# Sharing one pass through the output weights between a recurrent memory and its tokens

## The chip, the core and the metric

The kernel runs on one core of one Trainium2 chip. The metric is the time of one execution in microseconds (us) on the device. Each run was timed beside the kernel before on its own chip, and its ratio is to those runs. The experiments lie on three chips (runs 1 to 4, 5 to 8, 9 to 11); the kernel before differs by less than 0.2% between them, but a difference between runs of two groups, or from the changed kernel, is one across chips.

Engine names in the profile: PE is TensorE's matmuls, PEld its weight loads, DVE is VectorE, ACT is ScalarE, POOL is GpSimd, SP is SyncE, which starts most of the transfers here.

Tiles that the profiles name: `psm` holds the projections to queries and keys with which every segment starts, `psv` those to values, `psb` the query and key projections of a block's last tokens (eight per segment), `psS` the scores, `psD` and `psRt` the sums and reciprocals of the softmax, `psOm` and `psOt` the attention's output for memory and tokens, `pw` and `psy` (later `pwB`) the passes through `Wo`. `Rc` is the reciprocal and `PT` the probabilities, both made on DVE.

## The reference, cut to what matters

Two layers are applied twice: a recurrent attention with a small memory, and a gated MLP. All tensors are bf16. The attention is sequential: 64 segments of 32 tokens, and the 8 rows of memory that a segment starts with are the first 8 output rows of the segment before.

```python
# H = 32 heads, Dh = 128, Dm = 512, M = 8 memory rows, seg_len = 32
mem = mem0
for s in range(n_seg):                        # 64 segments, one after the other
    xs = x[:, s * seg_len:(s + 1) * seg_len, :]
    h = jnp.concatenate([mem, xs], axis=1)    # 40 rows
    q, k, v = (einsum('btd,dhe->bhte', h, W) for W in (Wq, Wk, Wv))
    p = softmax(where(mask, q @ k^T * scale, -1e9))
    o = einsum('bhqk,bhke->bhqe', p, v)
    o = einsum('bhte,hed->btd', o, Wo)        # Wo: 32 x 128 x 512
    mem = o[:, :M, :]                         # the next segment waits for this
    outs.append(o[:, M:, :])
...
x = x + A(layernorm(x)); x = x + B(layernorm(x))      # the whole pair twice
```

## The kernel before

Both recurrent stages (one per application of the attention) go through 16 blocks of four segments, 128 tokens to a block. The layer norm of a block is done once, and its rows are brought to the layout with the model dimension on partitions by PE transposes. `hA` holds the 8 memory rows and the first 24 tokens of a segment, `hB` and `hBs` the last 8 tokens.

The memory of a segment goes through `Wo` at once, because the next segment waits for it. The tokens are kept in `oT4` and go through `Wo` a block at a time, as filler work (`fill`) in the next block's segments.

```python
        def gen_block_ln(tb):
            xs = xp.tile([P, DM], F32, name="xs")                 # 2 buffers
            nc.sync.dma_start(xs[:], xd[tb * P:(tb + 1) * P, :])
            yield
            xn = wk.tile([P, DM], BF16, name="xn", bufs=1)
            nc.vector.tensor_scalar(out=xn[:], in0=xs[:], ...)    # layer norm
            ...
            for kt in range(KT):
                nc.tensor.transpose(pT[:, kt, :], xn[:, kt * P:(kt + 1) * P], ident_bf[:])
            ...                                                   # nine copies into hA, hBs, hB
            blk_state[tb] = dict(xs=xs, hB=hB)                    # xs held for gen_y

        def gen_y(tb):                                            # the tokens' pass through Wo
            psy = acc.tile([P, DM], F32, name="psy")
            for h in range(H):
                nc.tensor.matmul(psy[:, :], lhsT=bs["oT4"][:, h, :], rhs=Wo_sb[:, h, :], start=(h == 0), stop=(h == H - 1))
                if h % 4 == 3:
                    yield
            xo = xp.tile([P, DM], F32, name="xo", bufs=1)
            nc.vector.tensor_tensor(out=xo[:], in0=psy[:], in1=bs["xs"][:], op=ALU.add)
            nc.sync.dma_start(xd[tb * P:(tb + 1) * P, :], xo[:])
            _stats(nc, wk, xo[:], MV_out[:, tb, :])               # bn_stats for the next layer norm
```

```python
        # in segment(s): the memory's pass; column tile cg sums the heads h with h % 4 == cg
            for h in range(H):
                cg = h % 4
                nc.tensor.matmul(pw[32 * cg:32 * cg + 32, :], lhsT=uT_cur[:, h, :], rhs=Wo_sb[:, h, :],
                                 start=(h < 4), stop=(h >= H - 4), tile_position=(0, 32 * cg))
            nc.scalar.copy(pw_sb[:, 0:256], pw[:, 0:256])
            nc.vector.tensor_copy(pw_sb[:, 256:512], pw[:, 256:512])
            fill(FILLU)
            ...                                                   # token probabilities
            for kt in range(KT):
                nc.tensor.transpose(pmT[:, kt, :], pw_sb[:, kt * P:(kt + 1) * P], c["ident_f"][:])
            nc.vector.tensor_reduce(out=hA_nxt[:, :, 0:8], in_=...pmT..., op=ALU.add)   # sum of 4 partials
            ...                                                   # psOt, then copies into oT4
```

The softmax here doesn't subtract the row's maximum and nothing guards it: scores larger than these inputs give would overflow.

## Time and profile before

| what | value | from |
|---|---|---|
| time | 2544.65 us, median of 4 runs (2540.74 to 2553.52) | runs on the chip of the changed kernel |
| profiled span | 2520.7 us, of an execution some 22 us below the median | page |
| the two recurrent stages, first psm to last psm | 987.2 and 988.4 us | starts of psm in the trace |
| PE waits over 0.56 us in those stages | 42, together 34.4 us | from one matmul start to the next in the trace, each less 0.31 us |
| weight load and matmul pairs per segment | 332 | count in the trace |

Two rows of the page that the prediction did not use turn out to matter. The first is PE's granted clock in 40 slices, in tenths; the second is a DMA queue with its packets, megabytes, and share of time:

```profile
PEclk9999999999999999996999999999999999999999
...
q8 instruction: 350, 5.73, 1.0%
```

The clock is full except in the change between the stages. The `instruction` queue moved 350 packets; 5.73 MB over 350 is 16.4 KB each. The page's PE has 44,808 weight loads, so 89,616 loads and matmuls; over 350 that is 256.

And the first block of the first stage, in a table by window (window, its length, then busy time of PE, PEld, DVE, ACT and POOL with the count of instructions, then the granted clock, the DMA share and GB/s):

```profile
84.70:140.00 55.30, 53.94 (x1300) 28.06 (x1292) 30.99 (x69) 28.32 (x65) 5.22 (x14) 1.00 0.01 3
```

PE is busy 53.94 of 55.30 us at full clock: the first block runs as well as any later one (it lacks only the psy of a block before it).

### The profile page before, as it was taken

To read this page: it belongs to the slowest core of one execution; us is meant where nothing else is said; L and a number is where in the kernel's file an instruction comes from. 1 tells how busy PE (TensorE), PEld (TensorE's weight loads), DVE (VectorE), ACT (ScalarE), POOL (GpSimd) and SP (SyncE) were. 2 spreads that over 40 slices of the span, in tenths; PEclk is the share of its full clock that TensorE was granted. 3 is DMA by queue.
4 is the path that set the end of the run, shared out by engine and by line. 5 is a ranking of instruction groups with operands and counts; after the bars stand their busy time and mean duration, and the time that the engine had idled before them with its cause. 6 is when DMAs were issued, how large, how long until landed. Compare 5 with 4: busy or idle time off the path is not lost.

```text
span 2520.7 us, 96292 instructions
## 1 busy us (share of the span) xinstructions
PE 2260.2 (90%) x44720; PEld 1210.8 (48%) x44808; DVE 1162.1 (46%) x2582; ACT 986.6 (39%) x2242; POOL 201.5 (8%) x415
## 2 busy tenths in 40 slices
PE   0799999999999999981979999999999999999889
PEld 0344444444444444440754444444444444444466
DVE  2544444444444444460335444444444444444522
ACT  0344444444444444462004444444444444444700
POOL 1200000000000000001240000000000000000022
PEclk9999999999999999996999999999999999999999
DMA  9000000000000000038550000000000000000254
GB/s 366 11 11 11 11 11 11 11 11 11 11 11 11 11 11 11 7 114 229 137 170 11 11 11 11 11 11 11 11 11 11 11 11 11 11 11 23 98 130 105
DMA packets 105618, 107.94 MB, mean 43 GB/s; under 512 B 69776, under 2 KB 79360, under 8 KB 102144
## 3 DMA queue, kind: packets, MB, share of 16 engines
q1 hardware_dynamic: 79520, 46.88, 7.2%
q10 hardware_dynamic: 21728, 30.78, 3.5%
q0 software_dynamic: 3968, 24.12, 2.6%
q8 instruction: 350, 5.73, 1.0%
q14 instruction: 52, 0.43, 0.1%
HBM read 66.11 MB, written 18.87 MB: 34 GB/s over the span
## 4 chain that ended last, share of the span: by engine, by line
PE 76%; DVE 7%; ACT 6%; DMA 5%; issue 4%; POOL 1%; SPq 0%; ACTq 0%; POOLq 0%; DVEq 0%
PE psv L517 18%; PE psm L528 16%; PE pw L589 10%; PE psy L447 9%; PE pg L195 7%; PE psb L428 4%; ACT vs L522 3%; PE psS L549 3%; PE pmT L610 2%; DMA xs<-xd 2%; PE psRt L603 2%; DVE rowsB L436 2%; PE psOm L582 1%; PE py L206 1%; PE psOt L617 1%
## 5 line engine op out<-in xcount | busy, mean ns | idle before, releaser
L517 PE MATMUL psv<-Wv_sb,hBs 128*32 128x512 bf16 x4096 | 535.3, 381 | 0.0
L517 PE MATMUL psv<-Wv_sb,hA 128*32 128x512 bf16 x4096 | 534.6, 381 | 0.0
L531 ACT CAST rows<-psm 128x512 bf16<-128x512 f32 x512 | 300.1, 586 | 315.4 <-PE psm L528 315.4
L522 ACT CAST vs<-psv 128x512 bf16<-128x512 f32 x512 | 300.1, 586 | 153.7 <-PE psv L517 136.8
L528 PEld LDWEIGHTS <-hA 128*32 128x32 bf16 x8192 | 209.9, 97 | 240.3 <-DVE hA L612 25.2
L528 PE MATMUL psm<-Wq_sb,hA 128*32 128x512 bf16 x4096 | 266.3, 380 | 18.6 <-DVE hA L612 18.6
L528 PE MATMUL psm<-Wk_sb,hA 128*32 128x512 bf16 x4096 | 265.3, 379 | 0.0
L589 PE MATMUL pw<-Wo_sb,uT 128*32 128x512 bf16 x4096 | 244.6, 380 | 1.2
L517 PEld LDWEIGHTS <-hA 128*32 128x32 bf16 x4096 | 180.1, 95 | 108.0
L195 PE MATMUL pg<-wspT,z2n 128*128 128x256 bf16 (+1 forms) x1536 | 177.3, 277 | 59.6 <-issue 59.6
L447 PE MATMUL psy<-Wo_sb,oT 128*128 128x512 bf16 x962 | 223.0, 379 | 7.2 <-issue 4.8
L505 DVE STREAM_TRANSPOSE QQ<-rows 128x512 bf16<-128x512 bf16 x256 | 181.5, 709 | 79.2 <-ACT rows L531 74.8
L626 ACT CAST oT<-psOt 128x512 bf16<-128x512 f32 x128 | 75.0, 586 | 365.1 <-PE psy L447 230.2
L505 DVE STREAM_TRANSPOSE KK<-rows 128x512 bf16<-128x512 bf16 x256 | 181.6, 709 | 29.2 <-ACT rows L531 24.5
L195 PEld LDWEIGHTS <-z2n 128*128 128x128 bf16 (+1 forms) x1536 | 151.4, 100 | 85.2 <-issue 67.1
L517 PEld LDWEIGHTS <-hBs 128*32 128x32 bf16 x4096 | 180.1, 95 | 0.0
L447 PEld LDWEIGHTS <-oT 128*128 128x128 bf16 x1024 | 95.1, 98 | 120.5 <-issue 12.7
L490 POOL COPY QQ<-QTB 128x256 bf16<-128x256 bf16 x128 | 49.8, 404 | 1271.8 <-DVE QTB L438 1221.8
L589 PEld LDWEIGHTS <-uT 128*32 128x32 bf16 x4096 | 98.3, 96 | 104.8 <-ACT uT L585 21.8
L592 ACT COPY pw_sb<-pw 128x256 f32<-128x256 f32 x128 | 47.7, 373 | 236.4 <-PE pw L589 236.4
L198 DVE TENSOR_TENSOR gb<-pg,bsp_bc 128x256 f32<-128x256 f32 x96 | 40.7, 424 | 212.1 <-PE pg L195 212.1
L549 PEld LDWEIGHTS <-KK 128*32 128x32 bf16 x8192 | 89.7, 97 | 91.2 <-DVE KK L505 87.1
(104 smaller groups left out, 2540.7 us busy)
## 6 DMA issues: line engine op xcount, KB each, us to landing
xs<-xd SPq DMA_DIRECT2D x48, 256.0 KB, 3.4
xs<-xd ACTq DMA_DIRECT2D x48, 256.0 KB, 5.0
xd<-xo SPq DMA_DIRECT2D x32, 256.0 KB, 2.1
Wq_sb<-in_A_Wq_dram POOLq DMA_DIRECT2D x6, 1024.0 KB, 20.1
Wk_sb<-in_A_Wk_dram POOLq DMA_DIRECT2D x6, 1024.0 KB, 28.5
Wv_sb<-in_A_Wv_dram POOLq DMA_DIRECT2D x6, 1024.0 KB, 20.5
Wo_sb<-in_A_Wo_dram ACTq DMA_DIRECT2D x4, 1024.0 KB, 14.8
Wo_sb<-in_A_Wo_dram POOLq DMA_DIRECT2D x4, 1024.0 KB, 20.2
```

The costliest lines, as they stand in the source:

```text
L195: nc.tensor.matmul(pg[0:fsz, :], lhsT=z2n[:, st_i, f0:f0 + fsz], rhs=wspT[:, st_i, :], start=(st_i == 0), stop=(st_i == NT - 1))
L428: nc.tensor.matmul(psb[32 * cg:32 * cg + 32, :], lhsT=hB[:, kt, :], rhs=qk_rhs(j, kt, cg), start=(kt == 0), stop=(kt == KT - 1), tile_posi ...
L436: nc.vector.tensor_copy(rB[:], psb[:])
L447: nc.tensor.matmul(psy[:, :], lhsT=bs["oT4"][:, h, :], rhs=Wo_sb[:, h, :], start=(h == 0), stop=(h == H - 1))
L505: nc.vector.transpose(out=dst, in_=rows[j][:])
L517: nc.tensor.matmul(psv[32 * cg:32 * cg + 32, :], lhsT=(hA_cur if cg % 2 == 0 else hB_cur)[:, kt, :], rhs=Wv_sb[:, kt, col0:col0 + 512], st ...
L522: nc.scalar.copy(dstv, psv[:])
L528: nc.tensor.matmul(psm[32 * cg:32 * cg + 32, :], lhsT=hA_cur[:, kt, :], rhs=qk_rhs(j, kt, cg), start=(kt == 0), stop=(kt == KT - 1), tile_ ...
L531: nc.scalar.copy(r[:], psm[:])
L549: nc.tensor.matmul(psS[half][64 * g + 32 * part:64 * g + 32 * part + 32, hl8, :], lhsT=KK[:, part, half, 8 * g + hl8, :], rhs=QQ[:, :, hal ...
L589: nc.tensor.matmul(pw[32 * cg:32 * cg + 32, :], lhsT=uT_cur[:, h, :], rhs=Wo_sb[:, h, :], start=(h < 4), stop=(h >= H - 4), tile_position= ...
L626: nc.scalar.copy(oT4[:, 0:16, 32 * j4:32 * j4 + 32], psOt[0][:])
```

## The change

The intent is to let the tokens ride along in the memory's pass. `uT` has 32 columns per head, of which only 8 carried memory; now the other 24 carry 24 tokens of the segment before. For this, a column tile of PE no longer holds a quarter of the heads over 512 output columns, but all heads over a quarter of the output columns: 128 matmuls of 128 columns in place of 32 of 512. The result is 128x128, complete, and in a layout in which one predicated copy and one transpose on DVE make the next `hA`. The model dimension is permuted to fit, and the layer norm's rows go through DRAM to get that layout. The last 8 tokens of each segment get a pass per block (`pwB`). The rest of the token output is put together by transfers and an add on GpSimd.

```diff
+        def wo_pass(po, lhs):
+            for h in range(H):
+                for cg in range(4):
+                    nc.tensor.matmul(po[32 * cg:32 * cg + 32, 0:128], lhsT=lhs[:, h, :], rhs=wo_rhs(h, cg),
+                                     start=(h == 0), stop=(h == H - 1), tile_position=(0, 32 * cg))
+                if h % 8 == 7:
+                    yield
         def gen_block_ln(tb):
-            xs = xp.tile([P, DM], F32, name="xs")
+            xs = xp.tile([P, DM], F32, name="xs", bufs=1)
...
+            nc.sync.dma_start(xn_d[M + tb * P:M + (tb + 1) * P, :], xn[:])
             yield
+            for j4 in range(4):
+                t = prep.tile([P, P], BF16, name="pre")
+                nc.sync.dma_start(t[:], xn_d[t0:t0 + 32, :].rearrange("r (cg c) -> cg r c", cg=4))
+                pre[4 * tb + j4] = t
             yield
-            pT = acc.tile([P, KT, P], BF16, name="pT")            # PE transposes and copies go
+            ...                                                   # preB: the last 8 tokens of each segment
             hB = blkp.tile([P, KT, 32], BF16, name="hB")
+            nc.vector.transpose(out=hB[:].rearrange("p kt r -> p (kt r)"), in_=preB[:])
...
         def gen_y(tb):
-            psy = ...
+            pwB = acc.tile([P, DM], F32, name="pwB")
+            yield from wo_pass(pwB, bs["oB"])
+            ...                                                   # oB_sb, oB_d, loads of xs_y and ot_y
+            nc.gpsimd.tensor_tensor(out=xo, in0=xo, in1=xs[:], op=ALU.add)
+            nc.sync.dma_start(xd[tb * P:(tb + 1) * P, :], xo)
+            _stats(nc, wk, xo, MV_out[:, tb, :])
...
+        def build_hA(s, pw):
+            t = pre.pop(s)
+            if pw is not None:
+                nc.vector.copy_predicated(out=t[:], mask=maskM[:], data=pw[:, 0:128])
+            nc.vector.transpose(out=hA[s % 2][:].rearrange("p kt r -> p (kt r)"), in_=t[:])
...
         # in segment(s)
-            for h in range(H): ...                                # pw 512 wide, pw_sb
+            for _ in wo_pass(pw, uT_cur):
+                pass
+            build_hA(s + 1, pw)
+            store_o(s, pw)
             fill(FILLU)
...
-            ...                                                   # pmT transposes, tensor_reduce into hA_nxt
             psOt = ...
-            nc.scalar.copy(oT4[...]); nc.vector.tensor_copy(oT4[...])
+            for g, cp in ((0, nc.scalar.copy), (1, nc.vector.tensor_copy)):
+                cp(uT_nxt[:, 16 * g:16 * g + 16, 8:32], psOt[g][:, :, 0:24])
+                cp(oB[:, 16 * g:16 * g + 16, 8 * j4:8 * j4 + 8], psOt[g][:, :, 24:32])
```

## The prediction

> **What bounds the kernel now.** I read the busy table and the slices first, then the chain that ended last, then the groups by shape, then the chain in order of time within a few blocks.
>
> ```profile
> PE 2260.2 (90%) x44720; PEld 1210.8 (48%) x44808; DVE 1162.1 (46%) x2582; ACT 986.6 (39%) x2242; POOL 201.5 (8%) x415
> PE   0799999999999999981979999999999999999889
> PE 76%; DVE 7%; ACT 6%; DMA 5%; issue 4%; POOL 1%; SPq 0%; ACTq 0%; POOLq 0%; DVEq 0%
> ```
>
> PE is full in all slices but the start and the change between the two recurrent stages near the middle, and PE holds 76% of the chain. Nothing else is half busy. So a microsecond of PE work taken out of the recurrent stages is worth nearly a microsecond, if no wait opens in its place. Those stages are two times 16 blocks of four segments. The groups that the change touches:
>
> ```profile
> L589 PE MATMUL pw<-Wo_sb,uT 128*32 128x512 bf16 x4096 | 244.6, 380 | 1.2
> L612 DVE TENSOR_REDUCE hA<-pmT 128x32 bf16<-128x128 f32 x128 | 36.5, 285 | 119.0 <-PE pmT L610 119.0
> L610 PE MATMUL pmT<-ident_f,pw_sb 128*128 128x128 f32 x512 | 90.6, 287 | 4.6
> ```
>
> The reader sees that pw costs 8 groups of four column tiles per segment. The psy group (1,024 full matmuls, 962 recorded, 223.0 us busy) is the tokens' own pass through Wo. In order of time, the end of a segment that has no filler work in it:
>
> ```profile
> 642.65 1.94 PE pw L589 x32
> 644.59 0.02 issue
> 644.62 0.38 ACT pw_sb L592
> 645.00 0.04 issue
> 645.04 0.44 PE pmT L610 x2
> 645.48 0.22 PE psOt L617 x10
> 645.70 0.38 PE pmT L610 x2
> 646.08 0.02 issue
> 646.11 0.30 DVE hA L612
> 646.41 0.04 issue
> 646.45 3.64 PE psm L528 x64
> ```
>
> From pw's end to the next segment's psm the chain crosses four engines and takes 646.45 - 644.59 = 1.86 us. The last segment of the block before shows the psy pass:
>
> ```profile
> 658.21 3.19 PE psy L447 x14
> 661.40 0.44 PE pmT L610 x4
> 661.83 0.51 PE psOt L617 x32
> 662.34 0.16 issue
> 662.50 3.42 PE psy L447 x15
> ```
>
> In that stretch psm starts at 602.9, 618.8, 633.2, 646.45 and 665.8. The four segments of a block therefore take 15.9, 14.4, 13.3 and 19.4 us, together about 62.9 us. The 13.3 is the bare segment; the 19.4 holds psy; the 15.9 and 14.4 hold the four psb passes (16 matmuls in 0.87 us each, 3.5 us per block).
>
> [...] (1) [...] the starts of psm show groups of four, 3 to 4 ns apart within a group, and a new group each 216 ns. [...] psS has N=64 and a new weight load for each matmul, and 32 start in 0.24 us, 30 ns per group of four. (2) [...] The trace has 709 ns for 512 columns[...]. (3) [...] The trace has 285 (the reduce above) and 288 (the tensor_tensor on psD); I use 290. [...] (4)[...] The trace has 2.1 us for xd<-xo and 3.4 for xs<-xd on the same queue, so a round trip through DRAM is 5 us or so.
>
> **The change part by part.**
>
> *pw.* 32 matmuls of 512 columns become 128 of 128 columns: 32 groups of four at about 57 ns instead of 8 at 216. 32 x 57 = 1.82 us against 8 x 216 = 1.73. Even, or 0.1 us worse per segment. But it now carries 24 tokens of the segment before in the columns that were zeros, and yields one 128x128 tile.
>
> *psy.* Goes: 32 x 216 ns = 6.9 us per block, all on the path (PE is full around it). In its place the last 8 tokens of each segment, 32 per block, take a pwB pass: 1.8 us per block. Net -5.1, less 4 x 0.1 for pw: -4.7 us.
>
> *pmT, pw_sb, reduce.* Four fp32 transposes per segment (0.4 to 0.8 us of PE on the chain, 0.6 typical) go: 4 x 0.6 = -2.4 us per block. The block's pT transposes (4, 0.34 us) go too, into reads through DRAM.
>
> *The memory chain.* In place of the 1.86 us: predicated copy 0.29, transpose 0.31, three hand-overs of about 0.04 each: 0.72 us, both on one engine. psOt runs beside it (0.57 us in the timeline of PE, and a few tenths before matmuls of another form start). So in a bare segment 1.86 becomes 0.8, of which 0.6 has been counted as pmT. Further gain 0.5 us in the one bare segment of a block; in the others filler already covers the chain.
>
> *LN of the next block.* In the second segment psb waits for hB behind xn and nine small copies on DVE (PE psb waited 38.0 us in 30 places, 1.3 us each). xs no longer is held until psy is done, so the loads can be issued a block early. I take half: -0.6 us.
>
> *Added elsewhere.* About 22 small transfers per block on the SP queue (about 0.4 us of issue each, 9 of 55 us), an output copy on ACT, an add on GpSimd. ACT changes by about +0.05 us per segment: psOt's copy is split (+0.16) and o_sb comes (0.27), pw_sb goes (0.37). DVE is lighter: pw_sb, the reduce and eight hA/hBs copies go. Both stay near half busy.
>
> *Sum per block.* -4.7 - 2.4 - 0.3 - 0.5 - 0.6 = -8.5 us. I give back 0.5 for DVE standing in order behind a landing that comes later than planned (the hB transpose waits for a load, a store and a load). -8.0 x 32 = -256 us.
>
> *Ends.* Each recurrent stage has one more pw pass (1.8 us), and the last block's tokens go through DRAM, about 5 us, before the gMLP stage can take its statistics; against that the exposed psy of the last block (6.9 us) shrinks to 1.8. The first block needs the DRAM trip as well, but the GpSimd memsets covered that time (they end at 79.4 us, psb starts at 79.6). Estimate +3 us per stage, +6 in all. The permuted reads in the gMLP stage keep their element counts; 0.
>
> 2542.6 - 256 + 6 = about **2293 us**; the trace's bare-segment chain may be worth more than I took, so I put the point at **2285**.
>
> **Rivals.** *A: dispatch becomes the bound.* PE gets 240 more instructions per segment, and no burst of small matmuls in this trace is longer than 32, a pw pass is 128. [...] Against it: where a psS burst ends, at 1336.50, psv weight loads follow each other every 8.3 ns, each with its matmul in the stream; a group of four then needs 33 ns, below 57. [...] *C: a DMA wait takes psy's place.* The chain shows it already: DVE stood behind xn with xs landing at 670.97, and KK after it. Two such waits of 1 to 2 us per block would make it 2330 to 2370. For it: three DRAM trips in a row on one queue, and DVE in order. Against: pre has nine buffers and xs is free early, so it can run a block ahead. *D: the predicated copy is slow* (two passes, 0.6 us): +0.3 us per bare segment, +10 us, the rest hidden by filler. *E: DVE or ACT become the bound*: 46% and 39% busy and hardly changed; no.
>
> **Range and chances.** PE's own work alone gives -7.4 per block, about 2305; all waits removed (-9.5 per block) gives 2240; rival C gives up to 2370, of which I keep the lower half. Range 2235 to 2340. Faster by over 2% needs under 2492[...]: 0.96. Within 2%: 0.025. Slower: 0.015.
>
> **What would show it.** pw groups 57 ns apart and a pw pass near 1.8 us; psm about 12.2 us after psm in the bare segment, some 54.5 us per block; DVE predicated copy near 0.29 us and its transpose near 0.31; no psy and pmT rows; PE still near 90%. Wrong if pw's starts spread over 3 us or more (A, B), if DVE's idle time before hB, xn or the predicated copy sums over 60 us with a DMA as its end (C), or if the ends of the two stages cost over 10 us each.

## The result, and the profile after

The changed kernel takes 2446.39 us (median of 4 runs, 2444.18 to 2455.31). The ratio to the kernel before is 0.9626, with a 95% interval of 0.9586 to 0.9667. Ratios here are the mean time of one kernel's runs over the mean of the other's of the same rounds, so not quite the ratio of the medians. The change gains 98 us. The prediction had it gain 258, and its range ended at 2340: the direction was right, the time was 161 us above the point and outside the range.

The page of the changed kernel, rows of busy time, slices, clock, the instruction queue, and the chain that ended last:

```profile
PE 2063.5 (84%) x59776; PEld 1267.5 (52%) x59776; DVE 1111.9 (46%) x2425; ACT 987.0 (40%) x2404; POOL 270.3 (11%) x577
PE   0599999998999999773967988988899899997799
PEclk9999999999999999986989999999999999999899
...
q8 instruction: 467, 7.65, 1.3%
...
PE 63%; DMA 11%; DVE 9%; issue 7%; ACT 6%; SPq 2%; POOL 2%; ACTq 0%; POOLq 0%; DVEq 0%
```

PE has 197 us less work, but is down from 90% to 84%, and its share of the chain from 76% to 63%. DMA and "issue" have grown in the chain, and the clock has dips inside the stages. There are 59,776 matmuls and as many loads, 119,552 together, and the instruction queue has 467 packets: 119,552 / 467 = 256 exactly.

The parts themselves came out as predicted. The groups by shape (line, engine, operation, tiles, shape, count, then busy us, mean ns of one, and idle time before them with what ended it):

```profile
L475 PE MATMUL pw<-Wo_sb,uT 128*32 128x128 bf16 x16640 | 280.4, 226 | 34.0 <-issue 31.5
...
L544 DVE STREAM_TRANSPOSE hA<-pre 128x128 bf16<-128x128 bf16 x128 | 39.9, 311 | 4.7 <-DMA pre<-xn_d 0.5
...
L543 DVE CAST_PREDICATED pre<-maskM,pw 128x128 bf16<-128x128 uint16 x126 | 36.7, 291 | 199.3 <-PE pw L475 199.2
```

And the end of a bare segment in the chain (start, length, what), to be held against the six steps of the kernel before that took 1.86 us:

```profile
626.81 2.00 PE pw L475 x128
...
628.83 0.30 DVE pre L543
...
629.16 0.32 DVE hA L544
629.48 0.04 issue
629.52 3.64 PE psm L586 x64
```

From pw's end at 628.81 to the next psm at 629.52 are 0.71 us. So what went wrong lies between the parts. From the starts of psm, the length of each kind of segment (the n-th of a block) in the steady blocks of both stages:

| segment of the block | before, median | after, median (shortest) |
|---|---|---|
| first | 19.4 | 12.8 (12.2) |
| second | 15.8 | 15.0 (14.5) |
| third | 14.6 | 16.8 (15.3) |
| fourth | 13.3 | 14.3 (12.6) |
| sum | 63.0 | 58.9 (54.5) |

The steady blocks are the third to the fifteenth of each stage. The shortest sum to 54.5 us per block, the prediction's number, but in part by chance: the shortest third and fourth segments still hold waits (the tenth run below gets down to 53.4). The changed kernel seldom reaches these lengths. In the kernel before a kind of segment was the same every time, to 0.02 us in the first, third and fourth.

Three things take the time.

**Gaps in which PE waits for nothing that the profile shows.** The chain between two segments that carry filler:

```profile
655.64 0.22 PE psb L457 x4
655.86 0.76 issue
656.62 0.83 PE psb L457 x12
...
658.84 0.39 PE pwB L475 x20
659.24 1.12 issue
660.36 0.80 PE pwB L475 x44
```

PE stops in the middle of a run of identical matmuls, with no operand that the profile shows it waiting for, twice in 5 us (0.76 and 1.12 us). Nearly all gaps of this sort lie at one place in the count of PE's instructions, taken modulo 256: at 186 in the first stage, and 168 in the second. Between the two in this fence, from the gap at 655.86 to that at 659.24, PE issued 12 + 64 + 32 + 20 = 128 pairs, 256 instructions. There are 118 such gaps of 0.3 to 2.2 us in the two stages, together 124 us. 37 of them lie within pw, 34 within pwB, 20 within psOt, 14 within psm, 7 within psb and 6 between two tiles. In the kernel before there is none. The place will be called the mark.

**DVE standing in order.** Three rows of the table of waits (who, for what, us in total, times, longest):

```profile
DVE bnst L99 <- POOL ot_y L498: 88.8, 29, 17.2
...
DVE xn L424 <- DMA xs<-xd: 52.9, 29, 3.7
...
PE psD L632 <- DVE Rc L625: 31.7, 26, 3.0
```

bnst is the statistics of a block's output. It waits on DVE for GpSimd's add, and that add mostly waits for the last transfer into ot_y (22 of 32 times in the same table). What that does to PE, from the chain of one block's fourth segment:

```profile
607.79 1.27 POOL ot_y L498
...
609.08 0.69 DVE bnst L99
...
610.30 0.25 PE psD L632 x2
...
612.66 3.56 PE pw L475 x128
```

The softmax of the segment needs a reciprocal on DVE, which stands behind bnst, which stands behind GpSimd. PE stood still for 2.11 us before that psD. In the table above it waits for Rc 26 times, 31.7 us in all, 1.2 on the mean.

The row of xn is the layer norm. In the first block of the first stage DVE takes 13 of them, 12 of which wait for their load (22.6 us of waits in this window):

```profile
82.30:155.20 72.90, 57.71 (x1664) 33.05 (x1656) 35.63 (x78) 28.11 (x68) 6.86 (x22) 0.91 0.28 82
```

The window holds the four segments of the first block. They take 72.90 us where the kernel before took 55.30, with PE busy in 57.71 only; in the second stage it is 72.3 against 55.3.

**Half clock.** In the fence before last, pw takes 3.56 us, not 2.0. The records of the clock show half speed from 610.96 us for 6.83 us, just after that wait of 2.11 us; over the two stages of the changed kernel it is 64.8 us, and none in the kernel before. The two stages hold 16 such stretches of half clock, 13 of 3.41 us and 3 of twice that, 6.83; 3.41 us is called a window below. By the trace's ends of matmuls PE stood still for 1.1 to 3.0 us in the 3.41 us before each; but other windows with up to 1.8 us were not followed by half clock, so no threshold comes out. Before 13 of the 16 the longest wait of PE lies away from the mark; before the other 3 it is a gap at the mark.

### The profile page after: what moved, and what is told of

Its sections match the earlier page's. It is cut to its first block, busy times and chain, and to the rows that moved or that the text cites. A ratio compares the mean times of both kernels' runs of the same rounds, so it can differ in the third digit from the quotient of the medians.

```text
span 2442.4 us, 127869 instructions
## 1 busy us (share of the span) xinstructions
PE 2063.5 (84%) x59776; PEld 1267.5 (52%) x59776; DVE 1111.9 (46%) x2425; ACT 987.0 (40%) x2404; POOL 270.3 (11%) x577
## 4 chain that ended last, share of the span: by engine, by line
PE 63%; DMA 11%; DVE 9%; issue 7%; ACT 6%; SPq 2%; POOL 2%; ACTq 0%; POOLq 0%; DVEq 0%
PE psv L575 16%; PE psm L586 13%; PE pw L475 11%; PE pg L209 7%; ACT vs L580 3%; PE pwB L475 3%; DMA xs<-xd 3%; PE psb L457 3%; PE psS L607 3%; DMA wspT<-in_B_w_sp_dram 2%; DVE rowsB L465 2%; PE psRt L659 2%; DVE QTB L467 1%; DMA xb<-in_A_x_dram 1%; DMA oB_d<-oB_sb 1%
## 5 line engine op out<-in xcount | busy, mean ns | idle before, releaser
L586 PEld LDWEIGHTS <-hA 128*32 128x32 bf16 x8192 | 219.9, 98 | 238.9 <-issue 29.6
L475 PE MATMUL pw<-Wo_sb,uT 128*32 128x128 bf16 x16640 | 280.4, 226 | 34.0 <-issue 31.5
L586 PE MATMUL psm<-Wq_sb,hA 128*32 128x512 bf16 x4096 | 276.1, 385 | 21.2 <-DVE hA L544 13.2
L475 PEld LDWEIGHTS <-uT 128*32 128x32 bf16 x16640 | 249.9, 100 | 62.0 <-issue 38.8
L586 PE MATMUL psm<-Wk_sb,hA 128*32 128x512 bf16 x4096 | 274.9, 383 | 3.4 <-DVE rowsB L465 1.9
L575 PEld LDWEIGHTS <-hA 128*32 128x32 bf16 x4096 | 180.1, 96 | 109.9 <-issue 2.1
L548 ACT COPY o_sb<-pw 128x128 f32<-128x128 f32 x130 | 34.6, 266 | 352.3 <-DVE pre L543 334.4
L457 PE MATMUL psb<-Wq_sb,hB 128*32 128x512 bf16 x1024 | 71.3, 392 | 101.1 <-DVE hB L441 76.0
L457 PEld LDWEIGHTS <-hB 128*32 128x32 bf16 x2048 | 53.2, 99 | 145.5 <-DVE hB L441 76.0
L543 DVE CAST_PREDICATED pre<-maskM,pw 128x128 bf16<-128x128 uint16 x126 | 36.7, 291 | 199.3 <-PE pw L475 199.2
L673 ACT CAST uT<-psOt 128x384 bf16<-128x384 f32 x128 | 61.5, 480 | 149.0 <-PE psOt L667 149.0
```

The costliest lines, as they stand in the source:

```text
L457: nc.tensor.matmul(psb[32 * cg:32 * cg + 32, :], lhsT=hB[:, kt, :], rhs=qk_rhs(j, kt, cg), start=(kt == 0), stop=(kt == KT - 1), tile_posi ...
L475: nc.tensor.matmul(po[32 * cg:32 * cg + 32, 0:128], lhsT=lhs[:, h, :], rhs=wo_rhs(h, cg), start=(h == 0), stop=(h == H - 1), tile_position ...
L575: nc.tensor.matmul(psv[32 * cg:32 * cg + 32, :], lhsT=(hA_cur if cg % 2 == 0 else hB_cur)[:, kt, :], rhs=Wv_sb[:, kt, col0:col0 + 512], st ...
L586: nc.tensor.matmul(psm[32 * cg:32 * cg + 32, :], lhsT=hA_cur[:, kt, :], rhs=qk_rhs(j, kt, cg), start=(kt == 0), stop=(kt == KT - 1), tile_ ...
L673: cp(uT_nxt[:, 16 * g:16 * g + 16, 8:32], psOt[g][:, :, 0:24])
```

## The experiments

The theories. **Supply**: PE takes instructions faster than a block of 256 of them can be brought, now that each matmul is short. That PE's instructions come in such blocks is read from the instruction queue (350 packets of 16.4 KB before, 467 after, in both 256 of PE's loads and matmuls to a packet); that PE waits for them was conjecture, which e2 and e3 test. **Order**: DVE, in order, stands behind things that need a transfer, and the rest follows from that, half clock included. A third possibility was that the gaps are a matter of the transfers that the change adds.

All the runs passed the comparison with the reference. Two of them compute a wrong value on purpose (they use a wrong slice of the weights); that the comparison did not catch it means that it is a weak check of the attention's part, for the other runs too. Their times are of use, their results are not.

The kernel before, run along with them, had 2545.43 us (runs 1 to 4), 2545.10 (5 to 8) and 2541.79 (9 to 11).

| run | median us | ratio to before (95%) | gaps at the 256 mark: number, us | other PE waits over 0.56 us: number, us | half clock us |
|---|---|---|---|---|---|
| before | 2544.65 | | 0 | 42, 34.4 | 0 |
| after | 2446.39 | 0.9626 (0.9586 to 0.9667) | 118, 124.1 | 42, 54.0 | 64.8 |
| e1_stats_late | 2450.64 | 0.9639 (0.9610 to 0.9668) | 114, 117.4 | 44, 60.0 | 88.7 |
| e2_wo64 (wrong value) | 2339.07 | 0.9200 (0.9164 to 0.9235) | 0 | 49, 75.1 | 88.7 |
| e3_before_pw128 | 2626.91 | 1.0330 (1.0292 to 1.0367) | 66, 59.1 | 37, 28.1 | 34.1 |
| e4_spread_late | 2388.15 | 0.9388 (0.9347 to 0.9429) | 101, 96.4 | 24, 31.0 | 27.3 |
| e5_ln_anchor | 2465.51 | 0.9712 (0.9649 to 0.9775) | 109, 110.8 | 54, 75.8 | 85.3 |
| e6_stats_anchor | 2419.42 | 0.9529 (0.9459 to 0.9599) | 122, 136.0 | 28, 34.3 | 37.5 |
| e7_all3 | 2402.15 | 0.9463 (0.9404 to 0.9522) | 90, 76.4 | 31, 53.8 | 81.9 |
| e8_thin | 2357.04 | 0.9284 (0.9215 to 0.9353) | 80, 74.6 | 23, 24.4 | 34.1 |
| e9_after_all | 2371.01 | 0.9341 (0.9316 to 0.9366) | 125, 123.2 | 3, 1.5 | 6.8 |
| e10_wo64_all (wrong value) | 2237.96 | 0.8812 (0.8782 to 0.8843) | 0 | 6, 4.7 | 6.8 |
| e11_thin_hb | 2306.31 | 0.9093 (0.9055 to 0.9131) | 81, 67.8 | 2, 0.7 | 0 |

The three last columns are counted from the records of one profiled execution each, over the two recurrent stages: a gap is taken as one at the mark when it lies at the place modulo 256 at which most of the gaps between like matmuls of that stage lie. Gaps at the mark are those over 0.3 us from one matmul start to the next, less 57 ns each; other waits are counted from 0.56 us, less 0.31 us each.

### e2_wo64: half as many instructions for the same columns

```diff
         def wo_pass(po, lhs):
-            for h in range(H):
+            for h in range(0, H, 2):
                 for cg in range(4):
-                    nc.tensor.matmul(po[32 * cg:32 * cg + 32, 0:128], lhsT=lhs[:, h, :], rhs=wo_rhs(h, cg), ...)
+                    nc.tensor.matmul(po[32 * cg:32 * cg + 32, 0:256], lhsT=lhs[:, h, :],
+                                     rhs=Wo_sb[:, h:h + 2, :].rearrange("p h (kt g el) -> p g h kt el", kt=4, g=4)[:, cg], ...)
```

The same columns stream through PE, in 64 matmuls of 256 in place of 128 of 128, so the pass has 128 instructions in place of 256 (in the trace of e10, which has the same pass, it takes 1.93 to 1.96 us). The order on the other engines is as before; the sums are wrong.

> Wrong result on purpose. The changed kernel with each Wo pass made of 64 matmuls of 256 columns in place of 128 of 128: the same streaming time (16 groups of 110 ns, 1.76 us), half the instructions. Theory of instruction supply: the gaps at multiples of 256 PE instructions (about 111 us in 112 segments) fall under 40, the time falls by 60 to 110 us to 2336 to 2386. Rival (a wait for DMA and DVE alone explains the loss, or the small matmuls stream slower than 57 ns per group): within 15 us of 2446, or the pw group pace is seen to change.

It took 2339.07 us, 107 less than the changed kernel (2446.39) and within the expected range, and not one gap at the mark is left. The instruction queue has 386 packets, which is 98,816 / 256. This speaks for supply, and against the transfers, which are all still there. The other waits and the half clock grew (75.1 us and 88.7), so the 107 is not all that the gaps cost.

### e3_before_pw128: only the cutting of pw, in the kernel before

```diff
-            for h in range(H):
-                cg = h % 4
-                nc.tensor.matmul(pw[32 * cg:32 * cg + 32, :], lhsT=uT_cur[:, h, :], rhs=Wo_sb[:, h, :], ...)
+            for d4 in range(4):
+                for h in range(H):
+                    cg = h % 4
+                    nc.tensor.matmul(pw[32 * cg:32 * cg + 32, 128 * d4:128 * d4 + 128], lhsT=uT_cur[:, h, :],
+                                     rhs=Wo_sb[:, h, 128 * d4:128 * d4 + 128], ...)
```

The result is right, and nothing else of the change is in it: no added transfers, no moved work on DVE.

> The kernel before with its pw pass cut into four times as many matmuls of 128 columns each, nothing else. Result stays right. Streaming time 32 x 57 = 1.82 us against 1.73. Theory of instruction supply: PE instructions per segment go from about 700 to 890, the densest 256 of them take under 3 us, gaps appear at multiples of 256 instructions; 30 to 90 us slower than before, 2575 to 2635. Rival (128-column matmuls cost only their streaming): 2543 + 12, so under 2560.

It took 2626.91 us, 81 more than the kernel before on the same chip (2545.43), and within the expected range. From the chain:

```profile
636.06 0.30 PE psOt L619 x15
636.36 0.92 issue
637.28 0.39 PE psOt L619 x17
```

A gap within psOt, of the kind seen before, in a kernel that has none of the change's transfers; 66 of them, 59.1 us. So the denser instructions are enough to make the gaps. The pw pass itself takes 1.97 to 2.00 us here, and 1.91 to 1.94 in the kernel before. In the two profiles the stages grew by 73 us: 59 are the gaps, some 8 the longer pass (the shortest bare segment is 13.33 us against 13.27, and there are 128), and 6 are left for the half clock. The rest of the 81 us would lie outside the stages, in parts that this edit does not touch: they took 578 us in this profile and 545 in that of the kernel before, so a difference of this size there can't be read as the effect of an edit.

The half clock came here as well, 34.1 us of it, with no more of other waits than in the kernel before (28.1 us against 34.4). Each of its ten windows had a gap at the mark in the 3.41 us before it. So here half clock followed the gaps.

### e1_stats_late: the statistics a block later, by their place in the program

```diff
-            _stats(nc, wk, xo, MV_out[:, tb, :])
+            late.append(lambda: _stats(nc, wk, xo, MV_out[:, tb, :]))     # run in the next block's second segment
```

> One change to the changed kernel: the statistics of a finished token block (bn_stats on DVE) are emitted one block later, so that DVE does not stand in order behind the GpSimd add. Theory (two losses: DVE behind the GpSimd add, with PE idle and a slower clock after it; and PE running out of fetched instructions): about 1.2 us of wait per block goes, and the half clock after it, so 35 to 70 us less than the changed kernel's 2446: 2376 to 2411; the gaps ahead of the psD matmuls that wait for Rc, 31.7 us by the profile, fall under 5. Rival (only the instruction supply matters): within 10 us of 2446.

It took 2450.64 us, the same as the changed kernel. This tests nothing: although the place in the text was another, the built kernel had bnst at the same places in DVE's order in both stages (2,920 instructions, all in the same order but for two pairs of neighbours). It is a second run of the changed kernel, in effect, and shows how far the three columns of the table vary by themselves (half clock 64.8 and 88.7).

### e4_spread_late: the pwB pass between longer matmuls

```diff
+        def wfill():                                  # one step of pwB: two heads
+            ...
         # in emit_V, after each half of a psv, and after each psm
+                wfill()
         def fill(n):
-                for lst in (gens, ygen):
+                for lst in (gens,):
```

with the edit of e1. pwB's 128 matmuls no longer follow pw's 128; they lie, eight at a time, between matmuls of 512 columns.

> The late statistics of the first run, and the pwB pass emitted two heads at a time among the psm and psv matmuls instead of in bursts of eight heads after pw. Same instructions, thinner where they were dense. Theory of instruction supply: a further 30 to 70 us below the late statistics alone, 2320 to 2375, with fewer gaps at multiples of 256. Rival (supply is an average limit, or no limit): within 15 us of the first run.

It took 2388.15 us, 58 less than the changed kernel, and 13 over the expected range. The gaps at the mark fell from 118 to 101 and from 124.1 to 96.4 us. The same number of instructions, spread more thinly, costs less; but the gaps are only half of the 58 us, as the other waits fell to 31.0 us and the half clock to 27.3.

### e5_ln_anchor: the layer norm not ahead of its time

For this and the next, an instruction is held, in DVE's order, behind a given one (the last copy of the segment before).

```diff
+        def behind():
+            return tc.issue_after(last_dve[0].ins) if last_dve[0] is not None else nullcontext()
...
-            nc.vector.tensor_scalar(out=xn[:], in0=xs[:], ...)
+            with behind():
+                nc.vector.tensor_scalar(out=xn[:], in0=xs[:], ...)
```

> The changed kernel with each block's xn instruction on DVE held in its place in the instruction order (behind the last DVE copy of the segment before), so that the layer norms of later blocks no longer run ahead. Theory: the first block of each recurrent stage takes about 73 us against 55 of the kernel before because DVE stands in order behind 12 early xn, each waiting for its xs load; held, the first block falls to about 55, 15 to 20 us per stage: 2405 to 2420. Rival (the slow first block is the fetching of instructions or of weights): first block stays over 65 us, time within 10 of 2446.

It took 2465.51 us, 19 more than the changed kernel, where 26 to 41 less were expected. The first blocks are mended (54.3 and 54.7 us, from 72.9 and 72.3), which shows that the early layer norms were their cause. But the waits show what it opened:

```profile
DVE hB L446 <- DMA preB<-xn_d: 75.7, 32, 3.9
...
PE psOm L645 <- DVE PT L640: 44.2, 28, 3.0
```

With the layer norm later, the hB transpose, which needs a store of xn and a load of preB after it, now stands on DVE in every block (32 times), and the attention's PT behind it. The gain at the two starts was lost in the blocks.

### e6_stats_anchor: the statistics held as well as late

e1 with `with behind(): late.pop(0)()`, so that bnst does move.

> What the first run was meant to be: its edit did not move a single bn_stats in the DVE order. Here the statistics are held behind a DVE copy of the next block's first segment. Theory (DVE behind the GpSimd add stalls PE, and the half clock after it): the wait of psD for Rc falls from about 30 us to under 5 and the time by 30 to 60 us, to 2386 to 2416. Rival (the wait is hidden or another takes its place): within 12 us of 2446.

It took 2419.42 us, 27 less than the changed kernel and 3 over the expected range. PE's wait for Rc before psD fell from 31.7 us to 9.5. The other waits fell from 54.0 to 34.3 us and the half clock from 64.8 to 37.5; the gaps at the mark stayed (136.0). This cause is real, and smaller than the gaps.

### e7_all3: e4, e5 and e6 together

> Both holds and the thinner pwB of the fourth run together. If the three causes are separate losses, they add: 2388 (fourth run) less 30 to 40 for the first blocks, less what is left of the wait behind the statistics: 2330 to 2360. If they share one cause, near 2380.

It took 2402.15 us, 14 more than e4 alone and 42 over the expected range: the gains did not add. The hold of e5 brings its wait here too (DVE's hB transpose waits 82.5 us in 32 places; other waits of PE 53.8 us).

### e8_thin: small matmuls thinned further

e7, and: psOt goes into the next segment's psm, except in the fourth segment; pwB goes one head at a time from the first segment on; the layer norm runs two blocks ahead and is issued in the second segment; and the filler behind pw is set by hand (2, 2, 5 and 0 steps in the four segments).

```diff
-            yield from wo_pass(pwB, bs["oB"])
+            yield from wo_pass(pwB, bs["oB"], 1)
...
                 if ji == 1:
                     emit_T(0, 0)
+                    while pend_ot:
+                        pend_ot.pop(0)()              # psOt of the segment before
...
-            if j4 == 0 and tb + 1 < NB:
-                gens.append(gen_block_ln(tb + 1))
+            if j4 == 1 and tb + 2 < NB:
+                for _ in gen_block_ln(tb + 2):
+                    pass
```

> The seventh run, and: psOt of a segment goes into the next segment's psm (so that pw is not followed by another dense burst), one psb group stands behind pw to cover the memory chain, pwB is spread over three segments one head at a time. Theory of instruction supply: fewer gaps at multiples of 256 PE instructions, 20 to 50 us below the seventh run, 2285 to 2335. Rival (the burst of pw alone sets the gaps): within 15 us of the seventh run.

It took 2357.04 us, 45 less than e7 and 22 over the expected range; 80 gaps of 74.6 us. The gaps fell by 2 us only: the gain went with the other waits (53.8 to 24.4 us) and the half clock (81.9 to 34.1), so this run does not show that thinning cures the gaps.

### e9_after_all: the changed kernel with all three waits on DVE held

The changed kernel with the holds of e5 and e6, and a third on the hB transpose, which is issued two steps later as well. No matmul is moved for the sake of the gaps.

```diff
-            yield
+            for _ in range(3):
+                yield
             hB = blkp.tile([P, KT, 32], BF16, name="hB")
-            nc.vector.transpose(out=hB[:]..., in_=preB[:])
+            with behind():
+                nc.vector.transpose(out=hB[:]..., in_=preB[:])
```

> The changed kernel with three DVE instructions held in place and nothing else moved: xn (as in the fifth run), the statistics (as in the sixth), and the hB transpose, a segment after its loads are issued (in the fifth run DVE stood behind it for 1.7 us per block). Theory: the first blocks are 55 us (37 us less in all), the wait behind the statistics and behind hB are gone, with the half clock that followed them: 2365 to 2395, and about 120 us of gaps at multiples of 256 PE instructions remain. Rival (DVE order is not what costs): over 2420.

It took 2371.01 us, 75 less than the changed kernel, and within the expected range. The other waits are gone (1.5 us) and with them nearly all of the half clock (6.8 us are left, both stretches of it after a gap at the mark of 1.7 us). The first block, in the table by window:

```profile
80.90:134.50 53.60, 51.55 (x1664) 29.72 (x1656) 30.16 (x63) 27.89 (x68) 5.86 (x18) 1.00 0.04 10
```

PE is busy 51.55 of 53.60 us at full clock, with DVE at 63 instructions in place of 78. The gaps at the mark are as before (125, 123.2 us): the two causes are separate, and curing one leaves the other whole.

### e10_wo64_all: e9 with the pass of e2

> Wrong result on purpose (the Wo pass of 64 matmuls of 256 columns, second run), with the three holds of the ninth run. Closes the account: with the gaps of instruction supply and the waits of DVE both gone, the time should come near what the prediction worked out from PE's work, 2255 to 2295 (second run 2339 less 37 and less 15 to 45). If it stays over 2310, a further cause is open.

It took 2237.96 us, 133 less than e9 and 17 below the expected range. No gap at the mark is left, and a kind of segment is nearly the same each time (medians 12.15, 14.43, 14.64, 12.13). The chain's shares:

```profile
PE 72%; DVE 11%; DMA 7%; ACT 6%; issue 2%; POOL 1%; SPq 0%; ACTq 0%; POOLq 0%; DVEq 0%
```

"issue" is down from 7% to 2%. 133 us is about the 123 us of gaps that e9 had; of the other 10, the shorter pass may make some 7 (an estimate: the shortest first segment is 12.14 us against 12.18 in e9, and there are 162 passes). The values are wrong, so this is no kernel to use; it is the measure of what supply costs.

### e11_thin_hb: the best of the right ones

e8 with the hB transpose held, and issued two segments after its load.

```diff
             if j4 == 1 and tb + 2 < NB:
-                for _ in gen_block_ln(tb + 2):
-                    pass
+                ahead = gen_block_ln(tb + 2)
+                for _ in range(4):
+                    next(ahead)
+            if j4 == 3 and tb + 2 < NB:
+                for _ in ahead:
+                    pass
```

> The eighth run with the hB transpose held two segments after its loads are issued. Right result. Theory: its remaining DVE wait of 0.8 us per block goes, with half clock: 20 to 45 us below the eighth run's 2357: 2312 to 2337; the gaps of instruction supply, about 75 us, remain. Rival: within 10 us of 2357.

It took 2306.31 us (2300.70 to 2319.72), ratio 0.9093: 9% faster than the kernel before, 140 us faster than the change as it was made, and 6 below the expected range. By its edit it only moves instructions and leaves out none of the work. PE is at 88%, at full clock in both stages. Other waits fell to 0.7 us; 81 gaps of 67.8 us remain.

### How the gaps come about, as far as the records show

In the changed kernel's records of the instruction queue, the last packet to start before a gap, taken as the fetch of what PE goes on with, starts 0.2 to 1.8 us after PE has passed the mark before, half of them 0.7 to 1.2 us after it. PE goes on after a gap mostly 1.2 to 1.6 us after the transfer has ended, which is about 2.4 us after it started. From one mark to the next PE took 2.52 us at the least, and in no run with gaps less than 2.45. Between marks it is faster: a pw pass is 256 instructions (128 loads and 128 matmuls), and takes 1.97 us. In the kernel before, the shortest stretch of 256 took 4.0 us, and none stalled. On the mean the changed kernel has 4.2 us per 256 in the first stage and 4.4 in the second, enough if the fetches could run ahead; they behave as if only the next block were being brought. That they can't be further ahead is inferred from these times. Why is open, as is why the place modulo 256 differs between the stages.

## Why the prediction was wrong

**The steps that held.** pw: "32 groups of four at about 57 ns" is 56.4 in the trace, 14.1 ns a pair, and a pass 1.97 us from its first start to its last end (the trace before had not shown the 57). The memory chain: 0.72 us predicted, 0.71 found. Predicated copy 0.29 and transpose 0.31: 291 and 311 ns (the first was an estimate from the 285 and 288 of other instructions; the trace before had shown no transpose of this size, only 709 ns for 128x512). psy and pmT are gone. After psOt, "a few tenths before matmuls of another form start": 0.33 us from its last start to the first of psy in the trace before. Issue on SP, "about 0.4 us": 0.29 to 0.60 by line, in the median, in the trace after. "psm about 12.2 us after psm in the bare segment, some 54.5 us per block": the shortest lengths are 12.2 and, summed over the four, 54.5. "all waits removed (-9.5 per block) gives 2240": e10, which has nearly none, took 2238, with blocks of 53.4 us, and 62.9 - 9.5 is 53.4. That the times agree to 2 us is in part luck: e10's passes are shorter than those of the change by some 7 us, and the prediction's bounds of 2240 and 2305 leave out the 6 us of its own ends. The account of the work was right; what failed was what stands between the work.

**Rival A was put aside on the wrong evidence.** This is the step that failed. "where a psS burst ends, at 1336.50, psv weight loads follow each other every 8.3 ns [...] a group of four then needs 33 ns, below 57." The rate of dispatch is as read, and pw does run at 57 ns a group. But the limit, by the place of the gaps modulo 256, is on a quantity that this cannot show: time per 256 instructions. A burst of psS is 64 instructions, so the trace before had no stretch in which 256 came close together (shortest 4.0 us). The pass that the change adds is exactly 256. The prediction had even noticed that "no burst of small matmuls in this trace is longer than 32, a pw pass is 128", and took a rate seen over a short burst for a rate that lasts. Its sign of being wrong, "pw's starts spread over 3 us or more", came true in 13 of the 130 passes: 7 ran at half clock, and 6 held a gap at the mark. The usual pass spreads over 1.75 us; the loss is a gap, at most once in 256 instructions, and not a slower pace of each pair (rival B). Size: 123 us by the gaps, 133 us by e10 against e9. Put at zero.

**Rival C was there, and hardly counted.** "Two such waits of 1 to 2 us per block would make it 2330 to 2370." e9 shows what they cost: 75 us, or 2.3 us a block. The point took 0.5 us a block for it, 16 us in all. The sum was too small as well: two waits of 1 to 2 us in 32 blocks are 64 to 128 us, so 2349 to 2413 from the point. Its test (DVE's idle time before hB, xn or the predicated copy, with a DMA as its end, over 60 us) gives 8.8 + 52.9 = 61.7, just over. It missed the largest of the waits, bnst, because that one ends with GpSimd.

**A gain with the wrong sign.** "xs no longer is held until psy is done, so the loads can be issued a block early. I take half: -0.6 us." That hold was what had kept the layer norm at the pace of the blocks. Without it, thirteen ran in the first block, in DVE's order ahead of the attention's work: the first blocks of the two stages cost 17.5 and 17.0 us more than in the kernel before. e5 and e9 mend this by holding xn in its place.

**Half clock was not thought of.** The kernel before had none in its stages, and the prediction took the clock for given. Of its 64.8 us most came with the waits on DVE and went with them (6.8 in e9, none in e11); the rest followed gaps at the mark (3 of the 16 stretches), as all of it did in e3. Its share of the 75 us is at most half of that, 32 us (an estimate: all of PE's work in it taking twice as long, as pw's 3.56 us against 2.00 is nearly); no run has the change's waits without it.

**The ends.** Outside the two stages the profiled span grew by 14 us (545 to 559), with 6 predicted. Whether that is a miss is open: the same parts took 578 us in e3, which does not touch them.

The sum: 2446 - 75 (e9) - 133 (e10) = 2238, that is 47 us below the predicted 2285. The prediction's point lies 45 us above its own bound without waits, and the gaps and waits cost 208.

## What to carry to other kernels

Count instructions as well as columns: when a change cuts a matmul into narrower ones, look at how long the densest 256 instructions of PE will take, not only at how fast a short burst can go (here a pw pass of 256 took 1.97 us, and in no run with gaps did PE get from one mark to the next in less than 2.45), and spread dense passes between long matmuls (in e4 and e7 this took away 28 and 48 us of gaps). DVE stood in order here (behind bnst, which waited 88.8 us for GpSimd, PE waited 31.7 us for Rc; e6 took 22 of these away): so each instruction on it that waits for a transfer or for another engine needs a place in that order at which its data is surely there; a buffer that was held "too long" may be what kept it at that place. Short waits of PE can also cost the clock: in the changed kernel 1.1 to 3.0 us of standing still were followed by 3.41 or 6.83 us of half clock, 16 times in the two stages.
